# Spreading a row of maxima over all partitions: by way of DRAM instead of products with a diagonal

## The chip, the cores and the metric

The kernel runs on one core of a Trainium2 chip. The metric is the device time of one execution in microseconds; the time of a kernel is the median of several executions. A core has five engines that run their own instruction streams in order: PE (TensorE, matrix products), DVE (VectorE), ACT (ScalarE), POOL (GpSimd) and SP (SyncE), which here issues all DMAs.

## The reference

Linear attention (softmax of q over its channels, softmax of k over the sequence) is followed by a small network with the activation h - tanh(h). The inputs are q, k and v of 8 batches x 8 heads x 576 rows x 64 channels.

```python
k_s = k - np.max(k, axis=2, keepdims=True)          # over the sequence
k_s = np.exp(k_s)
k_s = k_s / (np.sum(k_s, axis=2, keepdims=True) + 1e-09)
kv = np.einsum('bhsd,bhse->bhde', k_s, v)
attn = np.einsum('bhsd,bhde->bhse', q_s, kv)        # q_s: softmax of q over d
x = attn.transpose(0, 2, 1, 3).reshape(B * S, H * D)  # 4608 x 512
h = x @ w_in                                         # 512 -> 2048
out = (h - np.tanh(h)) @ w_out                       # 2048 -> 512
```

For each batch the kernel needs the maximum over 576 rows for each of 8 x 64 = 512 columns of k, and this row of 512 numbers must stand in all 128 partitions before it can be subtracted.

## The kernel before, in words

The 4608 rows of x are cut into 9 chunks of 512. For each chunk j and each of 16 blocks f of d_ff there is a step: `ph` (12 products, x in a high and a low part against `w_i`), then the activation on ACT and DVE, ending in `gh` (ACT) and `gl` (POOL), and two steps later `po` (12 products of `gh` and `gl` with `w_o`, summed in PSUM over the 16 blocks). `ph` has two PSUM buffers, so the product of step n + 2 needs the DVE operation `t` of step n to be done.

Batches 0 and 1 and the weights are prepared under an order written out by hand (`ORDER`). From chunk 2 on, `prepare` lists the work that makes the x of a chunk and gives every piece a half step at which it is put into the program (`put(at, ...)`). There PE's and SP's order is the program's, while DVE's, ACT's and POOL's is set by a scheduler when the program is built. All engines work in order at run time: an instruction that waits holds up everything behind it on its engine, and on SP a DMA whose data aren't ready holds up all later DMAs.

For a batch b from 2 on the keys' softmax goes so: `k_load` brings k in two tiles of 256 rows and one of 64. `kv_max` (DVE) takes maxima down to a tile of 128 x 512. `kv_max_t` (PE) turns it (`pm`), `kv_row` (DVE) reduces to `mx`, 128 x 4: the 512 maxima lie down the partitions. `kv_row_h` and `kv_row_l` split `mx` into a rounded part `mh` and the rest `ml`. `kv_rows` spreads them: POOL multiplies the identity with `mh`, then with `ml`, to two tiles `d` of 128 x 512 with the numbers on a diagonal, and PE multiplies each with a matrix of ones, so that all partitions of the PSUM tile `pb` hold the row. `kv_sub` (DVE) subtracts `pb` from the three tiles of k, `kv_exp` (ACT) takes the exponent, and `kv_mm` (PE, `pk`) multiplies with v. At half step KX + 2 (= 3) of the chunk come `kv_max_t`, `kv_row`, `kv_row_h` and `kv_row_l`, at KX + 4 `kv_rows` and the subtractions.

The same DVE, POOL and SP also prepare q: `q_load`, `mq` (maxima, DVE), the subtraction (POOL, `q<-q,mq`), exponent (ACT), `sq` (sums, DVE), `qn` (POOL), then a turn on PE (`pt`) and `px`. The tile of q is single: the next `q_load` waits until the last `qn` has read it. v's first and second part share a buffer too: a memset on POOL that waits for the first `pk` products comes before the second `v_load`. The SBUF tag `qs` has three buffers, in which `km`, the two `d`, `qn` and `qs` follow one another. At the start of a chunk the four output tiles of the chunk before are copied by ACT and stored by SP (L680).

Of the kernel before, what the change touches and what calls it, by code (L numbers as in the profile page):

```python
# [10 lines left out]
F32 = mybir.dt.float32  # L11
F32R = mybir.dt.float32r
# [4 lines left out]
ALU = mybir.AluOpType  # L17
# [53 lines left out]
def attn_moe_kernel(  # L71
# [9 lines left out]
    nc = tc.nc  # L81
# [3 lines left out]
    P = 128  # L85
# [4 lines left out]
    NC = DM // P  # L90
# [15 lines left out]
    ap = ctx.enter_context(tc.tile_pool(name="ap", bufs=2))  # L106
    ps_o = ctx.enter_context(tc.tile_pool(name="ps_o", bufs=TPC, space=bass.MemoryType.PSUM))
    ps_h = ctx.enter_context(tc.tile_pool(name="ps_h", bufs=2, space=bass.MemoryType.PSUM))
    ps_m = ctx.enter_context(tc.tile_pool(name="ps_m", bufs=2, space=bass.MemoryType.PSUM))
# [4 lines left out]
    sm = ctx.enter_context(tc.tile_pool(name="sm", bufs=2))  # L114

    ident = const.tile([P, P], F32, name="ident")
# [2 lines left out]
    nc.gpsimd.tensor_copy(ident_r, ident)  # L119
    b_pa = sm.tile([P, 1], F32, name="b_pa")  # L120
    nc.gpsimd.memset(b_pa, PA)
    one = sm.tile([P, 1], F32, name="one")
    nc.gpsimd.memset(one, 1.0)
    one_r = sm.tile([P, 1], F32R, name="one_r")
    nc.gpsimd.tensor_copy(one_r, one)

    kvs = [const.tile([P, NC, D], F32, name=f"kvs{i}") for i in range(3)]

# [73 lines left out]
    def k_load(b: int, st: dict, u: int):  # L202
        if u < NKP:
            kt = ap.tile([P, H, 2, D], F32, name=f"k{b}_{u}", tag="k", bufs=NKP)
            src = k[b, :, 2 * P * u : 2 * P * (u + 1), :]
            nc.sync.dma_start(
                kt.rearrange("p h j d -> p h (j d)"), src.rearrange("h (p j) d -> p h (j d)", j=2)
            )
        else:
            kt = ap.tile([REST, H, D], F32, name=f"kr{b}", tag="kr", bufs=1)  # L210
            nc.sync.dma_start(kt, k[b, :, S - REST :, :].rearrange("h s d -> s h d"))
        st["k", u] = kt
# [30 lines left out]
    def kv_max(b: int, st: dict, n: int):  # L243
        if n == 0:
            st["km"] = km = ap.tile([P, H, D], F32, name=f"km{b}", tag="qs", bufs=3)
            kt = st["k", 0]
            nc.vector.tensor_tensor(km, kt[:, :, 0], kt[:, :, 1], op=ALU.max)
        elif n < 3:
            km = st["km"]
            nc.vector.tensor_tensor(km, km, st["k", 1][:, :, n - 1], op=ALU.max)  # L250
        else:
            km = st["km"][:REST]
            nc.vector.tensor_tensor(km, km, st["k", NKP], op=ALU.max)
# [20 lines left out]
    def kv_rows(b: int, st: dict):  # L274


        pb = ps_m.tile([P, NC, P], F32, name=f"pb{b}", tag="m")
        if b < 2:
            for a in range(NC):
                for n, m in enumerate((st["mh"], st["ml"])):  # L280
                    nc.tensor.matmul(
                        pb[:, a, :],
                        m[:, a : a + 1].broadcast_to([P, P]),
                        ident_r,
                        start=(n == 0),
                        stop=(n == 1),
                    )
        else:
            for n, m in enumerate((st["mh"], st["ml"])):
                d = ap.tile([P, NC, P], F32R, name=f"d{b}_{n}", tag="qs", bufs=3)  # L290
                nc.gpsimd.tensor_tensor(
                    d,
                    ident.unsqueeze(1).broadcast_to([P, NC, P]),
                    m.bitcast(F32).unsqueeze(2).broadcast_to([P, NC, P]),
                    op=ALU.mult,
                )
                nc.tensor.matmul(
                    pb.rearrange("p a m -> p (a m)"),
                    one_r.broadcast_to([P, P]),
                    d.rearrange("p a m -> p (a m)"),  # L300
                    start=(n == 0),
                    stop=(n == 1),
                )
        st["pb"] = pb.rearrange("p a (e d) -> p (a e) d", d=D)

    def kv_sub(b: int, st: dict, u: int):
        pb, kt = st["pb"], st["k", u]
        pb = pb.unsqueeze(2).broadcast_to([P, H, 2, D]) if u < NKP else pb[:REST]
        nc.vector.tensor_tensor(kt, kt, pb, op=ALU.subtract)

    def kv_exp(b: int, st: dict, u: int):
        nc.scalar.activation(st["k", u], st["k", u], AF.Exp)

    def kv_mm(b: int, st: dict, u: int):


        if u == 0:
            st["pk"] = ps_m.tile([P, NC, D + 2], F32, name=f"pk{b}", tag="m")
        kt, vt = st.pop(("k", u)), st.pop(("v", u))
        for j in range(2 if u < NKP else 1):  # L320
            for a, hh in [(a, hh) for a in range(NC) for hh in range(2)]:
                h = hh * NC + a
                nc.tensor.matmul(  # L323
                    st["pk"][hh * D : (hh + 1) * D, a, j : j + D + 1],
                    kt[:, h, j] if u < NKP else kt[:, h],
                    vt[:, h, j * (D + 1) : (j + 1) * (D + 1)],
                    start=(u == 0 and j == 0 and a == 0),
                    stop=(u == NKP and a == NC - 1),
                    skip_group_check=True,
                )  # L330

    def kv_den(b: int, st: dict, n: int):
        pk = st["pk"]
        if n == 0:
            st["sl"] = sm.tile([P, NC, 1], F32, name=f"sl{b}", tag="sl")
            nc.vector.tensor_scalar_add(st["sl"], pk[:, :, D + 1 : D + 2], EPS)
        elif n == 1:
            st["rs"] = sm.tile([P, NC, 1], F32, name=f"rs{b}", tag="rs")
            nc.vector.tensor_tensor(st["rs"], pk[:, :, 0:1], st["sl"], op=ALU.add)
        else:  # L340
            nc.vector.reciprocal(st["rs"], st["rs"])

    def kv_norm(b: int, st: dict):
        nc.vector.tensor_tensor(
            kvs[b % 3],
            st["pk"][:, :, 1 : D + 1],
            st["rs"].broadcast_to([P, NC, D]),
            op=ALU.mult,
        )
# [11 lines left out]
    def batches(i: int):  # L361
        (b, u), _ = tiles[i]
        return ((b - 1, 0, REST), (b, REST, P)) if u == "rest" else ((b, 0, P),)
# [146 lines left out]
    def prepare(j: int, put):  # L510

        mine = range(j * TPC, (j + 1) * TPC)
        new = {b for i in mine for b, _, _ in batches(i)}
        new -= {b for i in range(mine[0]) for b, _, _ in batches(i)}

        KX, PAIRS = 1, (16, 28)
        for b in new:
            st = {}
            for u in range(NKP + 1):
                put(0, lambda u=u: k_load(b, st, u))  # L520
            for u in (0, NKP):
                for part in (v_ones, v_load):
                    put(0, lambda u=u, part=part: part(b, st, u))
            for n in range(4):
                put(KX, lambda n=n: kv_max(b, st, n))
            for part in (kv_max_t, kv_row, kv_row_h, kv_row_l):
                put(KX + 2, lambda part=part: part(b, st))
            put(KX + 4, lambda: kv_rows(b, st))
            for u in range(NKP + 1):
                put(KX + 4, lambda u=u: kv_sub(b, st, u))  # L530
                put(KX + 4, lambda u=u: kv_exp(b, st, u))
            put(KX + 7, lambda: kv_mm(b, st, 0))
            for part in (v_ones, v_load):
                put(KX + 7, lambda part=part: part(b, st, 1))
            put(KX + 10, lambda: kv_mm(b, st, 1))
            put(KX + 10, lambda: kv_mm(b, st, NKP))
            for n in range(3):
                put(KX + 10, lambda n=n: kv_den(b, st, n))
            put(KX + 10, lambda: kv_norm(b, st))
        unit = None  # L540
        for i in mine:
            at = PAIRS[(i - mine[0]) // 2]
            turn = at - (3 if i % 2 else 5)
            if tiles[i][0] != unit:
                unit = tiles[i][0]
                if unit not in qs_of and tiles[i][1] == 0:
                    put(max(0, turn - 9), lambda unit=unit: q_load(unit))
                    put(max(2, turn - 4), lambda unit=unit: q_soft(unit))
            put(turn, lambda i=i: q_norm(i, nc.gpsimd))
            put(turn, lambda i=i: q_turn(i))  # L550
            put(turn, lambda i=i: q_keep(i))
            if i % 2:
                put(at, lambda i=i: x_mm(i - 1))
                for g in range(2):
                    for p in "hl":
                        put(at, lambda i=i, g=g, p=p: x_part(i - 1, g, p))
# [76 lines left out]
    dram = ctx.enter_context(tc.tile_pool(name="dram", bufs=1, space=bass.MemoryType.DRAM))  # L633
# [75 lines left out]
    for b in range(2):  # L709
        st = {}  # L710
# [43 lines left out]
    with tc.manual_schedule(engines={ENG.PE, ENG.DVE, ENG.Activation, ENG.Pool, ENG.SP}):  # L754
        for name in ORDER.split():
            eng = (nc.vector,) if name[-1] == "*" else ()
            name = name.rstrip("*")
# [74 lines left out]
```

## Time and profile before

| | us |
|---|---|
| median of 3 runs | 899.44 (899.38 to 899.83) |
| profiled execution, its time | 902.51 |
| its span in the trace | 900.7 |
| PE busy | 874.9 |
| DVE busy | 616.7 |
| ACT busy | 555.0 |
| POOL busy | 289.2 |

The profiled execution has a time of its own, and the trace covers its span. A busy time is the sum over an engine's instructions; PE's products overlap, so what one costs in a stream is the difference of two starts and not its duration. The row that a line of a timeline shows is: start, duration, engine, line, operation, output<-inputs, and in brackets the idle time before it and who ended it. L numbers are lines of the kernel before.

### The profile page before, as it was taken

Reading aid. Unit: us, or ns where it says so; the run is one execution under the profiler, and the core shown is the slowest. Engines: PE = TensorE matmul, PEld = TensorE weight load, DVE = VectorE, ACT = ScalarE, POOL = GpSimd, SP = SyncE. Lnnn points to the kernel's source line nnn. Section 1 sums busy time; section 2 is a strip of 40 time slices with the busy share of each in tenths; the row PEclk is TensorE's granted clock in tenths of the full one; section 3 lists DMA queues with packets and bytes.
Section 4 is the critical chain, followed back from the end, with each engine's and each line's share of the span. In section 5 each row is a group of like instructions: output and inputs, shape, how many; then the busy total and the mean of one; then the engine's idle time right before and its main releaser. Section 6 shows DMA issues by size and latency. Waiting matters only on the chain.

```text
span 900.7 us, 13173 instructions
## 1 busy us (share of the span) xinstructions
PE 874.9 (97%) x5008; PEld 716.6 (80%) x5008; DVE 616.7 (68%) x906; ACT 555.0 (62%) x967; POOL 289.2 (32%) x246
## 2 busy tenths in 40 slices
PE   5899989999999999999999999999999999999997
PEld 5777778878778888888888888888888888888886
DVE  7999988957576767567656865866765566454444
ACT  4899986655555657555646565565656566556553
POOL 4631112433144324332333332332433233222221
PEclk8999999999999999999999999999999999999999
DMA  9983301040142202300140011301100020001001
GB/s 292 306 314 118 115 9 41 24 140 2 53 100 61 69 1 82 107 24 1 47 123 7 24 47 35 107 0 48 48 24 1 1 70 12 1 1 48 1 1 47
DMA packets 79775, 57.47 MB, mean 64 GB/s; under 512 B 14688, under 2 KB 72032, under 8 KB 79712
## 3 DMA queue, kind: packets, MB, share of 16 engines
q1 hardware_dynamic: 79712, 56.63, 20.5%
q8 instruction: 39, 0.64, 0.3%
q14 instruction: 24, 0.20, 0.1%
HBM read 46.14 MB, written 10.49 MB: 63 GB/s over the span
## 4 chain that ended last, share of the span: by engine, by line
PE 78%; DVE 12%; ACT 5%; issue 2%; DMA 2%; POOL 1%; SPq 0%; DVEq 0%; ACTq 0%; POOLq 0%
PE po L651 36%; PE ph L568 36%; PE pk L323 2%; PE px L487 2%; PE pt L461 1%; DVE g L589 1%; DMA k<-in_k_dram 1%; DVE t L594 1%; DVE g L597 1%; DVE g L602 1%; ACT gh L605 1%; ACT mk L583 1%; DVE c_o L168 1%; DVE raw_i L157 1%; DVE c_i L168 1%
## 5 line engine op out<-in xcount | busy, mean ns | idle before, releaser
L651 PE MATMUL po<-w_o,gh 128*128 128x512 f32 x1152 | 358.7, 392 | 0.3 <-DVE w_o L179 0.2
L568 PE MATMUL ph<-xh,w_i 128*128 128x512 f32 x1152 | 313.4, 394 | 4.7 <-DVE t L594 2.3
L608 POOL TENSOR_TENSOR gl<-g,gh 128x512 fp32r<-128x512 f32 x128 | 171.5, 1340 | 389.3 <-ACT gh L605 367.0
L568 PEld LDWEIGHTS ph<-xh,w_i 128*128 128x128 f32 x1152 | 213.5, 188 | 49.8 <-DVE t L594 2.8
L651 PEld LDWEIGHTS po<-w_o,gh 128*128 128x128 f32 x1152 | 214.8, 188 | 47.3 <-issue 1.5
L589 DVE SCALAR_TENSOR_TENSOR g<-u,ph 128x512 f32<-128x512 f32 x144 | 98.2, 682 | 209.1 <-ACT t L583 204.7
L651 PE MATMUL po<-w_o,gl 128*128 128x512 f32 x576 | 224.5, 390 | 0.2 <-DVE gl L608 0.2
L605 ACT CAST gh<-g 128x512 fp32r<-128x512 f32 x144 | 89.5, 622 | 176.3 <-DVE g L602 168.5
L568 PE MATMUL ph<-xl,w_i 128*128 128x512 f32 x576 | 155.1, 391 | 0.0
L583 ACT ACTIVATE u<-ph 128x512 f32<-128x512 f32 x144 | 86.1, 598 | 78.4 <-PE ph L568 78.2
L597 DVE SCALAR_TENSOR_TENSOR g<-vv,g 128x512 f32<-128x512 f32 x144 | 117.4, 816 | 18.3 <-ACT vv L583 7.9
L651 PEld LDWEIGHTS po<-w_o,gl 128*128 128x128 f32 x576 | 108.3, 188 | 23.5 <-DVE gl L608 0.7
L568 PEld LDWEIGHTS ph<-xl,w_i 128*128 128x128 f32 x576 | 108.1, 188 | 23.7 <-DVE xl L508 0.5
L602 DVE COPY_PREDICATED g<-mk,t 128x512 f32<-128x512 int32 x144 | 119.6, 830 | 3.4
L583 ACT ACTIVATE mk<-ph 128x512 int32<-128x512 f32 x144 | 86.4, 600 | 36.1 <-DVE g L589 34.2
L583 ACT ACTIVATE vv<-u,b_pa 128x512 f32<-128x512 f32 x144 | 104.8, 727 | 0.7 <-DVE g L597 0.6
L594 DVE TENSOR_TENSOR t<-ph,t 128x512 f32<-128x512 f32 x144 | 98.0, 681 | 6.7 <-ACT mk L583 5.9
L583 ACT ACTIVATE t<-ph 128x512 f32<-128x512 f32 x144 | 85.6, 594 | 3.0 <-DVE g L589 3.0
L447 POOL TENSOR_TENSOR qn<-q,sq 128x512 f32<-128x512 f32 x30 | 34.6, 1153 | 27.7 <-PE pt L461 13.4
L413 POOL TENSOR_TENSOR q<-q,mq 128x1024 f32<-128x1024 f32 x14 | 28.0, 2003 | 46.4 <-DVE mq L408 44.6
L408 DVE TENSOR_REDUCE mq<-q 128x16 f32<-128x1024 f32 x15 | 18.3, 1217 | 23.3 <-DMA q<-in_q_dram 23.3
L179 POOL TENSOR_TENSOR w_i<-c_i,w_i 128x512 fp32r<-128x512 f32 x12 | 18.3, 1529 | 39.1 <-ACT w_i L175 39.1
(94 smaller groups left out, 577.4 us busy)
## 6 DMA issues: line engine op xcount, KB each, us to landing
k<-in_k_dram SPq DMA_DIRECT2D x16, 512.0 KB, 5.5
raw_i<-in_moe_w_in_dram SPq DMA_DIRECT2D x16, 512.0 KB, 6.7
raw_o<-in_moe_w_out_dram SPq DMA_DIRECT2D x16, 512.0 KB, 8.3
q<-in_q_dram SPq DMA_DIRECT2D x15, 512.0 KB, 3.9
v<-in_v_dram SPq DMA_DIRECT2D x14, 512.0 KB, 4.8
out_dram<-o SPq DMA_DIRECT2D x28, 256.0 KB, 2.2
kr<-in_k_dram SPq DMA_DIRECT2D x8, 128.0 KB, 5.2
spare_v<-in_v_dram SPq DMA_DIRECT2D x2, 512.0 KB, 7.9
```

What stands on the lines that cost most here:

```text
L179: eng.tensor_tensor(w[:, 1], st["c"].bitcast(F32), w[:, 0].bitcast(F32), op=ALU.subtract)
L413: eng.tensor_tensor(qf, qf, mq, op=ALU.subtract)
L447: eng.tensor_tensor(qn.rearrange("p a g d -> p g a d"), qt[:, :, j].rearrange("p (g a) d -> p g a d", g=2), sq[:, :, j : j + 1] .broadcast ...
L568: nc.tensor.matmul(ph, w[:, i, c], x[:, c, :], start=(n == 0), stop=(n == len(ops) - 1))
L583: nc.scalar.activation(new(tag, **of), st[src], fn, **kw)
L589: nc.vector.scalar_tensor_tensor(new("g"), st["u"], C2, st["ph"], op0=ALU.mult, op1=ALU.mult)
L594: nc.vector.tensor_tensor(st["t"], st["ph"], st["t"], op=ALU.subtract)
L597: nc.vector.scalar_tensor_tensor(st["g"], st["vv"], PB, st["g"], op0=ALU.add, op1=ALU.mult)
L602: nc.vector.copy_predicated(st["g"], st["mk"], st["t"])
L605: nc.scalar.copy(new("gh", F32R), st["g"])
L608: eng.tensor_tensor(new("gl", F32R), st["g"], st["gh"].bitcast(F32), op=ALU.subtract)
L651: nc.tensor.matmul(po[t], g[:, cols], wt["o", f][:, w], start=(begin and n == 0), stop=(end and n == 2),)
```

## The change

From batch 2 on the row of maxima is no longer made by POOL and PE. SP stores `mx` (128 x 4) to a DRAM tile `row` of 4 x 128, where the 512 numbers lie in order, and then loads this row into all partitions of an SBUF tile `rows`, 128 x 512. The load waits for the store. The split into `mh` and `ml` falls away for these batches, as do the two tiles `d`, the PSUM tile `pb` and the ones. Both DMAs are put at half step KX + 2, right behind `kv_row`. The subtractions read `rows` in SBUF instead of `pb` in PSUM. Batches 0 and 1 stay as they were.

```diff
-    one = sm.tile([P, 1], F32, name="one")
-    nc.gpsimd.memset(one, 1.0)
-    one_r = sm.tile([P, 1], F32R, name="one_r")
-    nc.gpsimd.tensor_copy(one_r, one)
...
     def kv_rows(b: int, st: dict):
-        pb = ps_m.tile([P, NC, P], F32, name=f"pb{b}", tag="m")
         if b < 2:
+            pb = ps_m.tile([P, NC, P], F32, name=f"pb{b}", tag="m")
...
         else:
-            for n, m in enumerate((st["mh"], st["ml"])):
-                d = ap.tile([P, NC, P], F32R, name=f"d{b}_{n}", tag="qs", bufs=3)
-                nc.gpsimd.tensor_tensor(
-                    d,
-                    ident.unsqueeze(1).broadcast_to([P, NC, P]),
-                    m.bitcast(F32).unsqueeze(2).broadcast_to([P, NC, P]),
-                    op=ALU.mult,
-                )
-                nc.tensor.matmul(
-                    pb.rearrange("p a m -> p (a m)"),
-                    one_r.broadcast_to([P, P]),
-                    d.rearrange("p a m -> p (a m)"),
-                    start=(n == 0),
-                    stop=(n == 1),
-                )
+            row = dram.tile([NC, P], F32, name=f"row{b}")
+            nc.sync.dma_start(row.rearrange("a p -> p a"), st["mx"])
+            pb = ap.tile([P, NC, P], F32, name=f"rows{b}", tag="qs", bufs=3)
+            nc.sync.dma_start(pb, row.unsqueeze(0).broadcast_to([P, NC, P]))
         st["pb"] = pb.rearrange("p a (e d) -> p (a e) d", d=D)
...
-            for part in (kv_max_t, kv_row, kv_row_h, kv_row_l):
+            for part in (kv_max_t, kv_row, kv_rows):
                 put(KX + 2, lambda part=part: part(b, st))
-            put(KX + 4, lambda: kv_rows(b, st))
```

The change also moves instructions on the engines that the scheduler orders. Three places follow; a number after a name tells apart tiles of one name, and L numbers of the program now are those of the changed kernel.

DVE at batch 7 (in chunk 6), from the maxima to the first operations of the step after. Before:

```order
L263 TENSOR_REDUCE mx_6095<-pm_6090 128x4
L594 TENSOR_TENSOR t_1_6051<-ph_1_6036,t_1_6051 128x512
L268 CAST mh_6097<-mx_6095 128x4
L602 COPY_PREDICATED g_1_6053<-mk_1_6057,t_1_6051 128x512
L272 TENSOR_TENSOR ml_6099<-mx_6095,mh_6097 128x4
L589 SCALAR_TENSOR_TENSOR g_2_6118<-u_2_6114,ph_2_6101 128x512
L597 SCALAR_TENSOR_TENSOR g_2_6118<-vv_2_6120,g_2_6118 128x512
L594 TENSOR_TENSOR t_2_6116<-ph_2_6101,t_2_6116 128x512
L309 TENSOR_TENSOR k_0_6007<-k_0_6007,pb_6149 128x1024
L309 TENSOR_TENSOR k_1_6009<-k_1_6009,pb_6149 128x1024
L309 TENSOR_TENSOR kr_6011<-kr_6011,pb_6149 64x512
L602 COPY_PREDICATED g_2_6118<-mk_2_6122,t_2_6116 128x512
```

Now, at the same place on DVE:

```order
L259 TENSOR_REDUCE mx_6056<-pm_6051 128x4
L578 TENSOR_TENSOR t_1_6012<-ph_1_5997,t_1_6012 128x512
L586 COPY_PREDICATED g_1_6014<-mk_1_6018,t_1_6012 128x512
L573 SCALAR_TENSOR_TENSOR g_2_6079<-u_2_6075,ph_2_6062 128x512
L581 SCALAR_TENSOR_TENSOR g_2_6079<-vv_2_6081,g_2_6079 128x512
L294 TENSOR_TENSOR k_0_5968<-k_0_5968,rows_6060 128x1024
L294 TENSOR_TENSOR k_1_5970<-k_1_5970,rows_6060 128x1024
L578 TENSOR_TENSOR t_2_6077<-ph_2_6062,t_2_6077 128x512
L294 TENSOR_TENSOR kr_5972<-kr_5972,rows_6060 64x512
L393 TENSOR_REDUCE mq_1_6220<-q_1_6092 128x16
L586 COPY_PREDICATED g_2_6079<-mk_2_6083,t_2_6077 128x512
```

The two large subtractions now stand ahead of the step's `t`, and `mq` ahead of the step's COPY_PREDICATED.

SP at batch 7, the stores of a finished chunk and what follows. Before:

```order
L680 DMA out_dram<-o_15_0_6069 128x512
L680 DMA out_dram<-o_15_1_6075 128x512
L680 DMA out_dram<-o_15_2_6081 128x512
L680 DMA out_dram<-o_15_3_6087 128x512
L393 DMA q_1_6131<-in_q_dram 128x8x128
L235 DMA v_1_6251<-in_v_dram 128x8x128
```

Now:

```order
L664 DMA out_dram<-o_15_0_6030 128x512
L664 DMA out_dram<-o_15_1_6036 128x512
L664 DMA out_dram<-o_15_2_6042 128x512
L664 DMA out_dram<-o_15_3_6048 128x512
L286 DMA row_6058<-mx_6056 128x4x1
L288 DMA rows_6060<-row_6058 128x512
L378 DMA q_1_6092<-in_q_dram 128x8x128
L231 DMA v_1_6205<-in_v_dram 128x8x128
```

The pair stands behind the four stores and ahead of the loads of q and v.

DVE at batch 2, from the subtractions on. Before:

```order
L309 TENSOR_TENSOR k_0_1691<-k_0_1691,pb_1838 128x1024
L309 TENSOR_TENSOR k_1_1693<-k_1_1693,pb_1838 128x1024
L309 TENSOR_TENSOR kr_1695<-kr_1695,pb_1838 64x512
L589 SCALAR_TENSOR_TENSOR g_14_1825<-u_14_1821,ph_14_1808 128x512
L408 TENSOR_REDUCE mq_0_1963<-q_0_1806 128x16
L597 SCALAR_TENSOR_TENSOR g_14_1825<-vv_14_1827,g_14_1825 128x512
```

Now:

```order
L294 TENSOR_TENSOR k_0_1687<-k_0_1687,rows_1788 128x1024
L294 TENSOR_TENSOR k_1_1689<-k_1_1689,rows_1788 128x1024
L294 TENSOR_TENSOR kr_1691<-kr_1691,rows_1788 64x512
L393 TENSOR_REDUCE mq_0_1952<-q_0_1802 128x16
L573 SCALAR_TENSOR_TENSOR g_14_1821<-u_14_1817,ph_14_1804 128x512
L581 SCALAR_TENSOR_TENSOR g_14_1821<-vv_14_1823,g_14_1821 128x512
```

`mq`, which waits for the load of q, now comes ahead of the step's `g`. On ACT in this place the order after q's exponent was `gh`, and is now `u`, `t`, `gh`. On POOL, `qn` loses the two `d` ahead of it. PE's order is the same but for the twelve products that fall away.

## The prediction

> **What bounds the kernel now.** I read the page's busy shares first, then the chain that ended last, then the busy times by stretch, and last the timelines around the places where a batch's maxima are spread.
>
> ```profile
> span 900.7 us, 13173 instructions
> PE 874.9 (97%) x5008; PEld 716.6 (80%) x5008; DVE 616.7 (68%) x906; ACT 555.0 (62%) x967; POOL 289.2 (32%) x246
> ...
> PE 78%; DVE 12%; ACT 5%; issue 2%; DMA 2%; POOL 1%; SPq 0%; DVEq 0%; ACTq 0%; POOLq 0%
> ...
> 150.00:200.00 50.00, 49.14 (x293) 40.15 (x291) 38.16 (x57) 29.81 (x52) 19.21 (x17) 1.00 0.18 53
> 250.00:300.00 50.00, 49.36 (x316) 40.02 (x315) 37.17 (x53) 28.61 (x48) 21.35 (x18) 1.00 0.36 92
> 600.00:700.00 100.00, 100.00 (x586) 81.95 (x586) 66.33 (x93) 59.55 (x102) 34.74 (x27) 1.00 0.09 27
> ```
>
> The first column of busy times in a stretch is PE's. Around batch 7 (600 to 700 us) PE is never idle; around batches 2 and 3 it idles 0.86 and 0.64 us. The clock granted is full in all three. So whatever leaves PE's stream shortens the program, as long as nobody makes PE wait in exchange. DVE, at 38 of 50 and 66 of 100 us, is the engine to watch: it works in order, and the change puts a DMA's landing in front of it.
>
> **What is removed from PE.** First the group, then batch 7 and batch 3 in PE's timeline (start, duration), the last line from the chain.
>
> ```profile
> L297 PE MATMUL pb<-d,one_r 128*128 128x512 f32 x12 | 4.1, 407 | 0.6 <-POOL d L291 0.6
> ...
> 632.91 0.63 PE L297 MATMUL pb<-d,one_r 128*128 128x512 f32 x2
> 633.38 1.09 PE L568 MATMUL ph<-xh,w_i 128*128 128x512 f32 x4
> ...
> 262.68 0.42 PE L297 MATMUL pb<-d,one_r 128*128 128x512 f32 x1
> 263.75 0.50 PE L297 MATMUL pb<-d,one_r 128*128 128x512 f32 x1 [0.64 <-POOL d L291]
> 264.24 2.74 PE po L651 x12
> ```
>
> The mean of 407 ns is no price: products overlap. In the stream a pair takes 633.38 - 632.91 = 0.47 us, and I use that for batches 2, 4, 5, 6 and 7: 5 x 0.47 = 2.35. In batch 3 PE waited for POOL's second diagonal between the two, so the pair cost 264.24 - 262.68 = 1.56. Together 3.91 us, all in a place where PE had other work ready behind.
>
> Batch 2 has a stall of its own, further down:
>
> ```profile
> 186.29 1.15 PE L323 MATMUL pk<-v,k 128*64 128x65 f32 x32 [0.86 <-POOL gl L608]
> 182.02 0.38 SPq L235 DMA_DIRECT2D v<-in_v_dram x1
> v<-in_v_dram SPq DMA_DIRECT2D x1, 512.0 KB, 4.2
> ```
>
> The releaser named is POOL's gl, but gl ended earlier; the load of v issued at 182.02 lands 4.2 later, at 186.2, and that is when the product starts. So the stall hangs on how early POOL gets to the memset that lets v be loaded. If that comes 1.33 us (0.86 + 0.47) earlier, the 0.86 goes too. The most that can be won is 3.91 + 0.86 = 4.77 us.
>
> **What is added: the time L from the issue of the first DMA to the landing of the second.** No transfer of 512 pieces of 4 bytes to DRAM, and no read of one 2 KB row by all partitions, is in the trace. The nearest issues from 100 to 700 us, by kind (last column: median us from issue to landing):
>
> ```profile
> out_dram<-o SPq DMA_DIRECT2D x18, 256.0 KB, 2.0
> out_dram<-o SPq DMA_DIRECT2D x4, 128.0 KB, 2.4
> q_rest<-in_q_dram SPq DMA_DIRECT2D x6, 128.0 KB, 3.2
> q<-in_q_dram SPq DMA_DIRECT2D x11, 512.0 KB, 3.9
> kr<-in_k_dram SPq DMA_DIRECT2D x6, 128.0 KB, 5.2
> ```
>
> Writing the maxima moves 8 KB. It is a store like out_dram, whose time hardly falls when its bytes are halved (2.0 and 2.4), so most of it is fixed: 2.0 below. Above, q_rest and kr have the same 512 pieces: 3.2, or 5.2 behind other loads. I take 2.2, since at this place only stores of the same kind stand in the queue. Reading it back is 256 KB in 128 rows of 2 KB: 2.0 below (a store of that shape), 3.9 above (a load of twice the bytes); I take 2.9. With two hand-overs of about 0.05, L = 5.2, bounds 4.1 and 9.2.
>
> By the Trainium skill ("DMA: Bandwidth & Descriptors", Anatomy of one DMA — SWDGE (gpsimd) path) a DMA costs about 2.0 us plus bytes at 436 GB/s; that gives an estimate of L = 4.6. The same page (Specifications) has pieces under 512 B done by read-modify-write, which speaks against this store; no row here shows a 4-byte store.
>
> **What L does in batch 7**, where four stores of outputs stand ahead on SP. DVE's, POOL's and SP's rows, and the product that needs the result:
>
> ```profile
> 626.04 3.04 SPq L680 DMA_DIRECT2D out_dram<-o  x4
> 627.62 0.69 DVE L263 TENSOR_REDUCE mx<-pm 128x4 f32<-128x512 f32 x1 [0.26 <-PE pm L259]
> 633.18 0.68 DVE L594 TENSOR_TENSOR t<-ph,t 128x512 f32<-128x512 f32 x1
> 633.79 2.33 DVE L309 TENSOR_TENSOR k<-k,pb 128x1024 f32<-128x1024 f32 x2
> 636.04 0.67 DVE L309 TENSOR_TENSOR kr<-kr,pb 64x512 f32<-64x512 f32 x1
> 636.64 0.75 DVE L602 COPY_PREDICATED g<-mk,t 128x512 f32<-128x512 int32 x1
> 637.29 1.20 DVE L408 TENSOR_REDUCE mq<-q 128x16 f32<-128x1024 f32 x1
> 638.62 1.91 POOL L413 TENSOR_TENSOR q<-q,mq 128x1024 f32<-128x1024 f32 x1 [4.21 <-DVE mq L408]
> 640.49 1.74 POOL L608 TENSOR_TENSOR gl<-g,gh 128x512 fp32r<-128x512 f32 x1
> 642.81 2.95 PE po L651 x12
> ```
>
> The maxima are ready at 628.31, but the last output's issue ends only at 629.08. So the rows arrive at x = 629.08 + L = 634.3, against 633.79 before. DVE's new order is k, k, t, kr, mq, then the copy. From start to start k, k take 2.25, t 0.61, kr 0.60, so mq starts at x + 3.46 and ends at x + 4.66; POOL subtracts until x + 6.7 and then makes gl, until x + 8.0 to x + 8.45 (1.3 alone, 1.74 in the row). ACT's gh is done before that. PE asks for this gl with its third product after 642.81, about 643.26, less the 0.47 saved: 642.8. So x may be 634.35 to 634.8, and L up to about 5.5 costs nothing; each further microsecond is one of PE. I replayed batches 3 to 6 in the same way and found them up to 0.8 us looser, so 5.5 for all five is on the safe side. SP itself loses nothing: behind the pair stands a load that POOL's qn let go only at 632.74 before.
>
> **What L does in batch 2**, where SP is free and the store goes out when the maxima are ready:
>
> ```profile
> 164.57 0.69 DVE L263 TENSOR_REDUCE mx<-pm 128x4 f32<-128x512 f32 x1
> 170.52 2.35 DVE L309 TENSOR_TENSOR k<-k,pb 128x1024 f32<-128x1024 f32 x2 [0.16 <-PE pb L297]
> 173.39 0.67 DVE L589 SCALAR_TENSOR_TENSOR g<-u,ph 128x512 f32<-128x512 f32 x1
> 175.21 1.22 DVE L408 TENSOR_REDUCE mq<-q 128x16 f32<-128x1024 f32 x1 [1.14 <-DMA q<-in_q_dram]
> 169.71 1.51 POOL L447 TENSOR_TENSOR qn<-q_rest,sq_rest 128x512 f32<-128x512 f32 x1
> 171.25 3.93 DMA q<-in_q_dram
> 176.00 0.60 ACT L583 ACTIVATE u<-ph 128x512 f32<-128x512 f32 x1 [0.42 <-PE ph L568]
> 176.49 0.59 ACT L583 ACTIVATE t<-ph 128x512 f32<-128x512 f32 x1
> ```
>
> x = 165.3 + L = 170.5, the same as before. What moves is the q load: it waited for POOL's qn, which stood behind the two diagonals (2.5 us). Without them q lands at about 172.7 and no longer holds up mq, which now comes straight after the three subtractions, at x + 2.87 = 173.4 instead of 175.21. From mq hangs the v load: POOL's subtraction, ACT's exponent, gh, gl, memset. ACT's new order puts two more steps (u and t, 0.5 each from start to start) ahead of gh. So v lands at 186.27 + (x + 2.87 - 175.21) + 1.0 = x + 14.9, and PE is there at 185.43 - 0.47 = 184.96. Up to L = 4.7 the stall is gone; at 5.2 half a microsecond of it stays.
>
> **Costed at nothing.** The casts and differences of the maxima (12 instructions on DVE) and the diagonals (12 on POOL): neither engine sets PE's pace at 600 to 700 us; what they won in batch 2 is in the sum through q. The memset and the cast of the ones at the start: I give them 0, or 0.3 us as the best case. One PSUM buffer less in use: I found no wait for it. The subtractions now read both operands from SBUF:
>
> ```profile
> 165.92 1.26 DVE L268 CAST mh<-mx 128x4 fp32r<-128x4 f32 x1
> 167.29 1.55 DVE L597 SCALAR_TENSOR_TENSOR g<-vv,g 128x512 f32<-128x512 f32 x1
> ```
>
> These two ran beside POOL's gl and diagonal. The second works on two operands in SBUF and took 1.55 us where t, with one operand in PSUM, takes 0.68 above: DVE's work on SBUF can stretch by 0.9 us while POOL runs. At the subtractions POOL has finished qn and waits for mq, so I take 0; the bound is 0.9 a batch, which counts as L + 0.9. The Trainium skill ("SBUF — State Buffer", SBUF: two separate sides) states the reason: a VectorE operation with two SBUF inputs and a GpSimd operation that reads SBUF exclude each other for a whole instruction. The two long rows fit that.
>
> **Sum.** Gain = 4.77 - max(0, L - 4.7) - 5 x max(0, L - 5.5). At L = 5.2 it is 4.77 - 0.5 = 4.3 us. The profiled execution, 902.51 us with its span of 900.7, stands 3.1 above the median of 899.44; the gain is a difference within it and I take it off the median: 899.44 - 4.3 = 895.2.
>
> **Rivals.**
> 1. The pair of DMAs is slow. For: 4-byte pieces, all partitions reading one row, kr at 5.2. Against: nothing else is in the queue, and 512 pieces in q_rest take 3.2 although two such loads run together. The gain is zero at L = 6.2; at L = 7 the sum is 4.77 - 2.3 - 7.5 = -5.0, 904.4 us. It decides through one mechanism: DVE stands at the subtractions, gl is late, PE waits, in every batch from 3 on.
> 2. L about 6, or the port stretches the subtractions by 0.9 at L = 5.2: the gain is 4.77 - 1.3 - 2.5 = 1.0, 898.5 us, no measurable change. If read-modify-write of pieces under 512 B, as the Trainium skill has it on the DMA page, adds a microsecond to the store, this is where it would end.
> 3. The products were free because the work behind them comes no sooner: 899.4. Against: PE has no idle time at 600 to 700 us and both neighbours of the pair start at once.
>
> **Chances.** A change below 0.2% (1.8 us), about what a measurement can tell from none, needs L between 5.9 and 6.5 or rival 3. Forecast, L up to 5.9: 0.72. Rival 2 with 3: 0.13 (0.09 and 0.04). Rival 1, L over 6.5: 0.15. The best case, L = 4.4, is 899.44 - 4.8 = 894.7, with 0.3 for the start 894.4, and I set the end at 894.3. Leaving out rival 1 and a sliver of the rest, the range ends at 899.5; the forecast's own range is 894.3 to 897.6.
>
> **What would show it.** After: no L297 group, no d on POOL; row landing at 2.0 to 2.5 and rows at 2.4 to 3.2; batch 7's first subtraction near 634.3 less what was won before; PE still idle-free at batches 4 to 7; the pk stall of batch 2 under 0.6. Wrong if PE shows waits for gl or for t in batches 3 to 7, if DVE's wait for rows is over 2 us, or if the subtractions take over 1.3 us each.

## The result and the profile after

The changed kernel takes 951.14 us (median of 4 runs, 947.79 to 951.90) against 899.63 (4 runs, 899.38 to 901.99): a ratio of 1.0555, interval 1.0539 to 1.057. It is 51.5 us slower; 895.2 was forecast and 899.5 was the end of the range. The profiled execution took 951.79 us with a span of 950.0.

First the page: busy times, the chain by engine, and the DVE group and the two DMA groups that are new (the store's row from the view of DMA issues, 100 to 800 us).

```profile
PE 887.3 (93%) x4996; PEld 724.7 (76%) x4996; DVE 610.8 (64%) x894; ACT 555.5 (58%) x967; POOL 271.3 (29%) x232
...
PE 69%; DMA 10%; DVE 9%; ACT 5%; issue 3%; SPq 2%; POOL 0%; ACTq 0%; DVEq 0%; POOLq 0%
...
L294 DVE TENSOR_TENSOR k<-k,rows 128x1024 f32<-128x1024 f32 x12 | 14.2, 1222 | 55.0 <-DMA rows<-row 55.0
...
rows<-row SPq DMA_DIRECT2D x6, 256.0 KB, 5.0
row<-mx SPq DMA_DIRECT2D x6, 2.0 KB, 8.3
```

The subtractions themselves take 1222 ns, as before. DVE idles 55.0 us ahead of them, 9.2 a batch, always for the load of the rows. The store of 2 KB lands after 8.3 us, the load after 5.0: L is 13.3, where 5.2 was forecast and 9.2 was the upper bound. DMA, 2% of the chain before, has 10% of it.

The waits, by engine (line waited for, total, times, longest), and PE's busy time in the stretches that were shown of before:

```profile
DVE k L294 <- DMA rows<-row: 55.0, 6, 9.7
PE ph L552 <- DVE t L578: 20.3, 4, 7.2
PE pk L308 <- ACT k L297: 18.7, 6, 7.0
...
150.00:200.00 50.00, 43.39 (x257) 35.47 (x256) 33.54 (x51) 25.20 (x44) 13.89 (x13) 0.93 0.11 32
250.00:300.00 50.00, 43.02 (x248) 35.26 (x248) 30.44 (x44) 23.21 (x39) 13.63 (x13) 0.90 0.30 76
600.00:700.00 100.00, 92.77 (x505) 75.64 (x504) 62.86 (x86) 55.71 (x96) 29.18 (x23) 0.97 0.19 51
```

PE, which never idled at 600 to 700 us, now idles 7.2 us there, and the clock granted (third number from the end) falls below 1.00 in each of the three stretches. Over the whole span PE idles 62.7 us (950.0 less 887.3) where it idled 25.8 before, and it is busy 12.4 us longer although it has twelve products fewer.

Batch 7 shows the whole of it: SP, DVE and PE.

```profile
669.86 0.41 SPq L286 DMA_DIRECT2D row<-mx  x1
678.21 0.33 SPq L288 DMA_DIRECT2D rows<-row  x1
...
668.28 0.69 DVE L259 TENSOR_REDUCE mx<-pm 128x4 f32<-128x512 f32 x1 [0.25 <-PE pm L255]
683.38 2.36 DVE L294 TENSOR_TENSOR k<-k,rows 128x1024 f32<-128x1024 f32 x2 [9.39 <-DMA rows<-row]
685.66 0.68 DVE L578 TENSOR_TENSOR t<-ph,t 128x512 f32<-128x512 f32 x1
...
686.40 2.07 PE L552 MATMUL ph<-xh,w_i 128*128 128x512 f32 x4 [7.23 <-DVE t L578]
```

The store is issued at 669.86; SP stands until 678.21 for its landing; the rows land at 683.3; DVE has stood since 674.0. The step's `t` stands behind the subtractions on DVE, and PE's product waits for `t`.

Why the store takes so long: busy share of the DMA engines (last but one) in the stretches after an issue at 163.69 (batch 2), whose landing lets SP go on at 171.83.

```profile
164.00:165.00 1.00, 1.00 (x6) 0.82 (x5) 0.63 (x2) 1.00 (x3) 0.74 (x1) 1.00 0.25 2
165.00:166.00 1.00, 1.00 (x7) 0.80 (x6) 1.00 (x1) 0.23 (x1) 1.00 (x2) 1.00 0.00 0
...
167.00:171.70 4.70, 4.70 (x23) 3.88 (x22) 0.61 (x1) 1.71 (x3) 1.30 (x2) 1.00 0.00 0
```

The last number is GB/s: the 2 KB are moved within 1.3 us of the issue. Then the profile shows no busy DMA engine for over 6 us until the landing is reported. So the time doesn't go into the moving of the pieces, but into what follows until the landing is reported. The Trainium skill ("DMA: Bandwidth & Descriptors", Anatomy of one DMA — SWDGE (gpsimd) path) says of the fixed cost that it is mostly the receipt of the write, which can be surprisingly long towards HBM. That section is about DMAs issued by GpSimd, and this one is issued by SP; the trace fits it in kind, with some 6 us in place of the page's 2.0, but it doesn't show what this time is spent on.

### The profile page after: what moved, and what is told of

Its sections match the earlier page's. It is cut to its first block, busy times and chain, and to the rows that moved or that the text cites. A ratio compares the mean times of both kernels' runs of the same rounds, so it can differ in the third digit from the quotient of the medians.

```text
span 950.0 us, 13133 instructions
## 1 busy us (share of the span) xinstructions
PE 887.3 (93%) x4996; PEld 724.7 (76%) x4996; DVE 610.8 (64%) x894; ACT 555.5 (58%) x967; POOL 271.3 (29%) x232
## 4 chain that ended last, share of the span: by engine, by line
PE 69%; DMA 10%; DVE 9%; ACT 5%; issue 3%; SPq 2%; POOL 0%; ACTq 0%; DVEq 0%; POOLq 0%
PE po L635 33%; PE ph L552 32%; DMA row<-mx 4%; DMA rows<-row 3%; PE pk L308 2%; PE px L472 1%; PE pt L446 1%; DVE k L294 1%; DMA k<-in_k_dram 1%; DVE t L578 1%; DMA raw_o<-in_moe_w_out_dram 1%; DVE g L573 1%; DMA raw_i<-in_moe_w_in_dram 1%; DVE g L581 1%; DVE g L586 1%
## 5 line engine op out<-in xcount | busy, mean ns | idle before, releaser
L635 PE MATMUL po<-w_o,gh 128*128 128x512 f32 x1152 | 363.3, 397 | 3.4 <-ACT gh L589 3.1
L552 PE MATMUL ph<-xh,w_i 128*128 128x512 f32 x1152 | 316.2, 397 | 22.7 <-DVE t L578 20.3
L592 POOL TENSOR_TENSOR gl<-g,gh 128x512 fp32r<-128x512 f32 x128 | 169.5, 1324 | 440.4 <-ACT gh L589 418.0
L635 PEld LDWEIGHTS po<-w_o,gh 128*128 128x128 f32 x1152 | 217.7, 191 | 51.2 <-ACT gh L589 3.5
L635 PE MATMUL po<-w_o,gl 128*128 128x512 f32 x576 | 227.5, 395 | 0.5 <-DVE gl L592 0.2
L581 DVE SCALAR_TENSOR_TENSOR g<-vv,g 128x512 f32<-128x512 f32 x144 | 119.5, 830 | 17.9 <-ACT vv L567 7.5
L586 DVE COPY_PREDICATED g<-mk,t 128x512 f32<-128x512 int32 x144 | 116.8, 811 | 3.6
L297 ACT ACTIVATE k<-k 128x1024 f32<-128x1024 f32 x16 | 16.9, 1056 | 62.2 <-DVE k L294 61.9
L294 DVE TENSOR_TENSOR k<-k,rows 128x1024 f32<-128x1024 f32 x12 | 14.2, 1222 | 55.0 <-DMA rows<-row 55.0
```

The lines of the kernel that those rows point to most:

```text
L552: nc.tensor.matmul(ph, w[:, i, c], x[:, c, :], start=(n == 0), stop=(n == len(ops) - 1))
L581: nc.vector.scalar_tensor_tensor(st["g"], st["vv"], PB, st["g"], op0=ALU.add, op1=ALU.mult)
L586: nc.vector.copy_predicated(st["g"], st["mk"], st["t"])
L592: eng.tensor_tensor(new("gl", F32R), st["g"], st["gh"].bitcast(F32), op=ALU.subtract)
L635: nc.tensor.matmul(po[t], g[:, cols], wt["o", f][:, w], start=(begin and n == 0), stop=(end and n == 2),)
```

## The experiments

Each was compared with the kernel before on the same chip: 900.59 us (15 runs) for e1 to e4, 900.73 (15) for e5 to e8, 901.24 (9) for e9 and e10, 900.98 (21) for e11 and e12.

### The store and the load by themselves (e1_probe, e8_stores)

To the kernel before, chains of DMAs are added on SP in stretches in which it has nothing to do. No engine waits for them; each overwrites or reads the tile of the one ahead, so that the next issue shows when the one ahead landed. Two of the stores, as an example:

```diff
+    t = store("sta", [NC, P], lambda t: t.rearrange("a p -> p a"), dt[:, :NC])  # 512 x 4 B, adjacent
+    go(dt, t.rearrange("a p -> (a p)").unsqueeze(0).broadcast_to([P, DM]))
+    store("std", [P, NC, 16], lambda t: t[:, :, 0:1], dt[:, :NC].unsqueeze(2))  # 512 x 4 B, 64 B apart
```

> The kernel before, with chains of extra DMAs on SP in the quiet stretches after the loads of k (nobody waits for them but the next DMA of the chain). Stores from SBUF to DRAM: sta 512 pieces of 4 B to neighbouring addresses as in the change; stb 128 pieces of 16 B; std 512 pieces of 4 B, 64 B apart; ste 512 of 4 B, 512 B apart; stf 512 of 64 B; sti 512 of 256 B; sth 128 of 4 B; stg 4 of 512 B; stc 128 of 2 KB. Loads of 128 x 2 KB: one row for all partitions (fresh from sta, stb, stg; old; from the input k) and 128 different rows. Theory A, pieces under a line's size are written by read-modify-write and neighbours in one line wait for each other: sta 8.3, stb 2 to 4, std and ste 2 to 3.5, sth 3 to 8, the others about 2. Theory B, each piece under 512 B costs by itself whatever its place: sta, std, ste, stf all 7 to 8.5, stb and sth 3 to 4. Theory C, any small store to DRAM is acknowledged late: all of them near 8 but stc. Loads: if one row read by all partitions is what makes 5.0, every broadcast takes about 5 and different rows 2.5 to 3; if it is that the row was just written, only the fresh ones do. Time: 899 to 901, no change, if DMAs off the path cost nothing.

> The kernel before, with chains of DMAs that nobody waits for, in stretches in which SP has nothing to do; the time stays at about 900.6. Theory C (small pieces that go to the same 64 bytes of DRAM are written one after another, about 0.45 us each): 512 pieces of 4 bytes land in 4 to 5 us when they lie 8 bytes apart, 2.5 to 3.2 at 16 and 2.2 to 3.1 at 32; 16 adjacent pieces of 4 bytes take 7 to 8, as 256 do; 128 pieces 64 bytes apart 2 to 2.5; 256 pieces of 8 bytes, adjacent, 4 to 5. Theory D (each piece under 512 bytes has a price): the time goes by their number, 16 pieces about 2, 512 pieces about 8 at every distance. The load that reads a row just stored takes about 5 us by both, and a load of other data behind such a store about 3.

Measured: e1_probe 900.79 us (10 runs), ratio 1.0005, interval 0.9992 to 1.0017: this traffic alone costs nothing that the runs can tell. e8_stores ran once, at 902.08, which decides nothing about the time; only its landings are used. SP's timeline of the first, then of the second (there a digit at the end of a name is left out: `sp` is 512 pieces 8 bytes apart, `s` 16 adjacent pieces, `sother` and `sagain` 512 adjacent ones):

```profile
297.05 0.37 SPq L520 DMA_DIRECT2D sta<-probe  x1
305.74 0.34 SPq L527 DMA_DIRECT2D probe<-sta  x1
310.79 0.33 SPq L520 DMA_DIRECT2D stb<-probe  x1
...
477.92 0.32 SPq L520 DMA_DIRECT2D stg<-probe  x1
479.11 0.35 SPq L544 DMA_DIRECT2D probe<-stg  x1
```

```profile
298.95 0.37 SPq L520 DMA_DIRECT2D sp<-probe  x1
302.33 0.34 SPq L534 DMA_DIRECT2D probe<-in_k_dram  x1
...
378.79 0.34 SPq L520 DMA_DIRECT2D s<-probe  x1
380.26 0.35 SPq L542 DMA_DIRECT2D probe<-in_k_dram  x1
...
581.26 0.37 SPq L520 DMA_DIRECT2D sother<-probe  x1
591.83 0.34 SPq L557 DMA_DIRECT2D probe<-in_k_dram  x1
594.94 0.37 SPq L520 DMA_DIRECT2D sagain<-probe  x1
```

The store of the change lands after 305.74 - 297.05 = 8.7 us, and later after 10.6; four pieces of 512 bytes (`stg`) after 1.2. All of them, from such differences:

| store to DRAM | us |
|---|---|
| 512 x 4 B, adjacent | 8.4 to 10.6 (4 times) |
| 256 and 128 x 4 B, adjacent | 7.7 and 7.1 |
| 16 x 4 B, adjacent | 1.5 |
| 512 x 4 B, 8, 16, 32, 64, 512 B apart | 3.4, 2.8, 2.1, 3.0, 2.2 |
| 128 x 4 B, 64 B apart | 1.5 |
| 256 x 8 B and 128 x 16 B, adjacent | 3.3 and 2.5 |
| 512 x 64 B and 512 x 256 B | 2.5 and 1.9 |
| 4 x 512 B | 1.2 |
| 128 x 2 KB | 2.0 |

(The stores 64 and 512 bytes apart also lie in another order: a partition's four pieces follow one another.) The number of pieces doesn't set the price, and neither does their size by itself: 512 pieces of 4 bytes cost 2.1 us at 32 bytes apart. Of the forms tried, only many pieces of 4 bytes that touch each other are slow. In e1_probe theory A met nearly all its times; B fell with the spread pieces, C with the 16-byte and 512-byte ones. In e8_stores theory C had 16 adjacent pieces, one block of 64 bytes, at 7 to 8 us; they took 1.5, so it fell in that form. Theory D had 512 pieces at about 8 us at every distance, and fell with those apart. What happens in the memory stays open, also for theory A, whose mechanism no run shows. As for the load, one row to all partitions takes 310.79 - 305.74 = 5.05 us when it was just stored in this way (4.1 and 5.4 in the second kernel), but 3.1 when it is one that nobody wrote (594.94 - 591.83, right behind such a store) or was stored long before (3.2; 4.5 once, behind loads of v), and 3.1 and 3.0 when it was just stored as 128 pieces of 16 bytes or 4 of 512. So reading what was just written in adjacent 4-byte pieces costs 1 to 2 us more.

### Stores of larger pieces (e4_16, e6_turn)

e4_16 stores 128 pieces of 16 bytes, which leaves the row in another order, so that every subtraction is done in two parts. e6_turn turns the maxima on PE first:

```diff
-            row = dram.tile([NC, P], F32, name=f"row{b}")
-            nc.sync.dma_start(row.rearrange("a p -> p a"), st["mx"])
+            turned = ps_m.tile([NC, P], F32, name=f"turned{b}", tag="m")
+            nc.tensor.transpose(turned, st["mx"], ident)
+            line_of = sm.tile([NC, P], F32, name=f"line{b}", tag="line", bufs=1)
+            nc.vector.tensor_copy(line_of, turned)
+            row = dram.tile([NC, P], F32, name=f"row{b}")
+            nc.sync.dma_start(row, line_of)
```

> The changed kernel with one thing changed: the maxima are stored as they lie, 128 pieces of 16 B, and the subtraction (two instructions in place of one) reads the row in the other order. Theory A: the store falls from 8.3 to 2 to 4, L from 13.3 to 7 to 9, and the time to 905 to 920. Theory C: 945 or more.

> The changed kernel, but the maxima are first turned by one small product on PE and copied to 4 partitions, so that the store moves 4 pieces of 512 bytes in place of 512 of 4. Theory A (the store of small neighbouring pieces is what is slow): the store lands in under 1.5 us, the load in 3 to 5, L is 4.5 to 6.5 behind the copy, DVE waits 0 to 3 us at a batch's subtractions, and the time is 898 to 912 us. Rival (a store to DRAM that is read back at once is slow whatever its pieces): the store takes 5 us or more, and the time is over 925.

Measured: e4_16 918.44 us, ratio 1.0197 (1.0169 to 1.0226); the store lands after 2.0, the load after 4.3, DVE waits 13.6 us in all, and its subtractions take twice 1.07 us in place of once 1.22. The time lies within theory A's range, the store at its lower end and L = 6.3 below its 7 to 9; the loss of 17.9 us is more than the 13.6 of waiting, and the doubled subtractions are what else the edit adds. e6_turn 900.91 us, ratio 1.0003 (0.999 to 1.0016). Its waits and loads, and its PE at 600 to 700 us:

```profile
DVE k L298 <- DMA rows<-row: 11.1, 6, 4.5
...
rows<-row SPq DMA_DIRECT2D x6, 256.0 KB, 3.8
...
600.00:700.00 100.00, 100.00 (x588) 81.87 (x586) 66.93 (x91) 59.02 (x102) 31.19 (x25) 1.00 0.10 30
```

The same way through DRAM, with the same read right behind the write, costs nothing once the store's pieces are large. Theory A held but for DVE's waits in batches 2 and 3 (4.3 and 4.5 us where it had at most 3; 0.3 to 0.8 in the others). The loss is gone, and DVE's wait for the rows fell from 55.0 to 11.1. The order made at build differs too: the subtractions stand a few operations later on DVE, but by an estimate from batch 7, a pair of 13.3 us would leave DVE standing for 9 us there too (store issued at 629.46, DVE free at 633.4). With store and load at 1.2 and 3.8, L is 5.0, near the forecast's 5.2; but the forecast's gain of 4.3 us isn't there.

### The removal alone (e2_none)

```diff
-            nc.sync.dma_start(row.rearrange("a p -> p a"), st["mx"])
-            nc.sync.dma_start(pb, row.unsqueeze(0).broadcast_to([P, NC, P]))
+            st["pb"] = ident[:, :D].unsqueeze(1).broadcast_to([P, H, D])
```

> The changed kernel without the spreading: neither DMAs nor products; a part of the identity is subtracted instead of the maxima, and the rest stays. It measures the term of the sum for what was removed: the prediction's 4.8, so 894.7 (893.5 to 896). Rival, the products were free: 899.4. If the slower time of the changed kernel came from DVE's new order and not from the landing, this would stay above 920.

Measured: 903.70 us (6 runs, 901.31 to 907.86), ratio 1.004 (1.0014 to 1.0066): nothing to wait for, and still no gain. It is even 3.1 us slower; the profiled execution, 901.49, is one of the fastest, so the trace may not show all of that. Where `pk` of batches 5 and 7 starts in the kernel before, then in e2_none, then e2_none's new waits of PE at 150 to 180 us:

```profile
450.25 1.15 PE L323 MATMUL pk<-v,k 128*64 128x65 f32 x32
641.66 1.15 PE L323 MATMUL pk<-v,k 128*64 128x65 f32 x32
```

```profile
450.07 1.15 PE L306 MATMUL pk<-v,k 128*64 128x65 f32 x32
640.67 1.15 PE L306 MATMUL pk<-v,k 128*64 128x65 f32 x32
...
PE po L633 <- POOL gl L590: 1.6, 1, 1.6
PE po L633 <- ACT gh L587: 1.3, 1, 1.3
```

A batch takes 191.41 / 2 = 95.7 us before and 190.60 / 2 = 95.3 without the products: 0.4, near the 0.47 of the forecast. What doesn't come is the rest. The subtractions no longer depend on the maxima here, and at batch 2 they stand ahead of them on DVE (155.08 and 159.81, `mx` at 162.98), between the operations of a step and before its COPY_PREDICATED. PE stands 2.9 us there for `gh` and `gl`, for which it didn't wait before. The 0.86 us for the load of v is gone, as forecast. So this run has a DVE order of its own: it prices the removed products, but not the order of the changed kernel.

### The same slow pair, out of the way (e3_late, e5_early, e9_hidden, e11_hidden456)

If DVE's standing is the whole cost, it must go when the pair of 13.3 us lies ahead of need. e3_late holds the subtractions and q's maxima behind a later step; e5_early makes the maxima four half steps sooner and holds the subtractions in their old place; e9_hidden also clears SP's queue; e11_hidden456 does so for batches 4 to 6 alone. The core of them:

```diff
+        with tc.issue_after(copied[-1]):   # behind the COPY_PREDICATED of the latest step
             nc.vector.tensor_tensor(kt, kt, pb, op=ALU.subtract)
...
-                put(KX, lambda n=n: kv_max(b, st, n))
+                put(KX - 4, lambda n=n: kv_max(b, st, n))
-                put(KX + 2, lambda part=part: part(b, st))
+                put(KX - 2, lambda part=part: part(b, st))      # turn, reduce, store
+            put(ROWS, lambda: kv_rows(b, st, 1))                # the load: e9, e11
```

> The changed kernel with both DMAs, but the subtractions, and the maxima of q that wait for a load behind the pair on SP, are held behind a later step's copy on DVE (about 15 us after the maxima in place of 5), and the products with v four half steps later. Theory, the whole loss is the wait for the landing in DVE's order: back to 894 to 897, with DVE's wait for rows under 1 us a batch, and PE busy 100% in the stretches of batches 4 to 7. Rival, the DMAs cost by themselves (SP held, contention): 920 or more.

> Batches 0 to 2 as before. From batch 3 on the keys' maxima, their store and the load of the rows are put four half steps earlier, and the subtractions are held by an order on DVE behind the step in which they stood before, so that at least 13 us lie between the store's issue and their place. Theory A (all that the change costs is that DVE stands at the subtractions until a pair of 13.3 us has landed): DVE's wait for rows falls from 55.0 us to under 5 in all, PE is idle-free again at batches 4 to 7, and the time is 896 to 902 us: 900.6 less at most 5 x 0.47, give or take 3 for the other order. Rival B (the subtractions from SBUF, the traffic of the pair or the queue behind it cost time of their own): over 915 us with no wait for rows.

> As e5_early, with SP's queue cleared around the pair: the loads of v's first and last part and of the chunk's first q come ahead of the store of the maxima, and the load of the rows is put two half steps behind the store, so that SP doesn't stand for the landing. The subtractions are held three steps (some 17 us) behind the maxima, against 13.3 us for the slow pair. Theory A (the pair costs what waits for it and nothing else): DVE waits under 5 us in all for rows, mq for q under 20, PE is idle-free at batches 4 to 7 and a batch takes 95.2 to 95.4 us from pk to pk in place of 95.7; the time is 897 to 901.5 us. Rival B (the pair, or reading the rows from SBUF, has a cost of its own): over 905 us.

> As e9_hidden, for batches 4, 5 and 6 alone, in which e9_hidden showed no wait for the rows; batches 2, 3 and 7 are spread by products as in the kernel before. Theory A (the slow pair costs only what stands for it): no wait for rows, no wait of more than 1 us on PE in batches 4 to 6, and the time is that of before less up to 3 x 0.4: 898.5 to 901.5 us. Rival B (the pair or the operands in SBUF have a price of their own, or SP's queue lets something else wait): 903 us or more.

Measured: 947.86 us (ratio 1.0529, 1.0497 to 1.0561), 961.50 (1.0679, 1.0665 to 1.0694), 925.82 (1.0269, 1.0252 to 1.0286) and 901.98 (1.0014, 1.0005 to 1.0023). The first three missed what theory A expected, and their times lie where the rivals had them. The main waits of each, in this order (before, DVE waits 23.3 us for q in the whole span, 4.6 at most at once):

```profile
DVE k L300 <- DMA rows<-row: 0.9, 1, 0.9
PE pt L453 <- POOL qn L439: 34.2, 10, 6.4
```

```profile
DVE mq L421 <- DMA q<-in_q_dram: 59.3, 12, 14.7
PE po L669 <- ACT o L696: 26.8, 6, 8.8
...
SPq L277 <- DVE mx L263: 194.8, 5, 53.6
SPq L279 <- DMA row<-mx: 41.1, 5, 8.5
```

```profile
DVE mq L424 <- DMA q<-in_q_dram: 37.3, 12, 16.1
PE ph L590 <- DVE t L616: 11.1, 3, 8.0
PE pm L259 <- DVE km L253: 6.3, 1, 6.3
```

```profile
row<-mx SPq DMA_DIRECT2D x3, 2.0 KB, 8.6
PE po L674 <- ACT o L701: 0.8, 2, 0.6
```

In none of them does DVE wait for the rows any more (0.9 us in all in e3_late), so the wait itself was moved each time; it came back elsewhere. In e3_late q's maxima, held with the rest, made `qn` late, and PE waits for it. In e5_early SP stands first until the maxima are there (53.6 us once) and then for the landing, and the load of q and the stores of outputs stand behind it: DVE waits for q, and PE waits for the copies of outputs (`o`), whose buffers the stores hold. In e9_hidden this is left in batch 3 (16.1 us), and in batch 7 PE waits 2.7 us for `k`; in 4 to 6 there is no wait of a microsecond on PE. e11_hidden456 keeps only those three: with a store that still lands after 8.6 the loss of some 9 us a batch is gone from each of them, and 1.0 us (0.45 to 2.1) over before is left, some of it 0.8 us in which PE waits for `o`. It is half a microsecond over the range that theory A gave; rival B's 903 isn't reached. The 1.2 us that its removed products should have given are missing too, so the three hidden pairs cost some 2 us. So a transfer of 13.6 us can be hidden almost free, though it pays in SP's queue as well as on DVE.

### Is the half clock a cost of its own? (e7_fill, e10_fill)

```diff
+            fill = {3: 25, 4: 16, 5: 25, 6: 9, 7: 25}     # e7_fill: 64, 42, 64, 24, 64
+            if b in fill:
+                put(KX + 6, lambda: warm(fill[b]))        # products of the identity with itself
             put(KX + 7, lambda: kv_mm(b, st, 0))
```

> The changed kernel with 64, 42, 64, 24 and 64 products of the identity with itself (about 0.088 us each, 22.7 us in all; their result is not used) on PE ahead of the place at which it waits in batches 3 to 7. Theory A (an idle PE is granted half the clock for some microseconds afterwards): the products fill most of the idle time, the clock stays at 1.00 behind them, the 32 products of pk take about 1.15 us in place of 2.00, and the time falls by 8 to 16 us to 935 to 943. Rival B (the clock falls for another reason, or there is no more to gain than idle time): the time stays at 948 to 953 or grows, and pk still takes 2.00.

> As e7_fill, with the fillers' number set by what one takes there (0.226 us): 25, 16, 25, 9 and 25 products in batches 3 to 7, 22.6 us in all, within the idle time. Theory A (an idle PE is granted half the clock afterwards): the same waits end as before, but the products behind them run at full clock; the time falls by 6 to 12 us, to 939 to 945, although PE has more to do. Rival B: 948 or more.

Measured: 967.19 us (ratio 1.074, 1.0723 to 1.0758) and 953.47 (1.0582, 1.0565 to 1.0599). In e7_fill one product took 0.226 us and not 0.088 (64 of them 14.45; the profile counts each as two), so it filled too much. PE at batch 3, in the changed kernel and then in e10_fill:

```profile
280.77 2.00 PE L308 MATMUL pk<-v,k 128*64 128x65 f32 x32 [6.98 <-ACT k L297]
...
281.00:282.00 1.00, 1.00 (x22) 1.00 (x22) 1.00 (x2) 1.00 (x2) 0.00 (x0) 0.50 0.00 0
```

```profile
275.48 5.74 PE L196 MATMUL warm<-ident 128*128 128x128 f32 x50
282.69 1.15 PE L308 MATMUL pk<-v,k 128*64 128x65 f32 x32 [1.47 <-ACT k L297]
287.65 1.21 PE L555 MATMUL ph<-xh,w_i 128*128 128x512 f32 x4 [0.82 <-DVE t L581]
```

After 7 us of idling the clock granted is 0.50 and the 32 products take 2.00 us; with the fillers it is 1.00 and they take 1.15, as before the change. So idling does cost the clock. The Trainium skill ("TensorE: Matmul & The Clock Gate", Part 1: The HAM clock gate) has the same, half rate after an idle window of about 3.4 us; in the traces looked at here each idle time from 3.8 us on did it, and of shorter ones some (2.38 and 2.72 in e9_hidden) and others not (2.81 in the changed kernel, 3.53 in e10_fill). But the time didn't fall: 953.5 against 951.1, with ratios to before whose intervals overlap. Two limits: the mean clock came back only from 0.969 to 0.982 (0.994 before), and DVE's wait for the rows was 58.4 us in e10_fill's trace, 3.4 more than in the changed kernel. So a gain of up to some 3 us may be hidden there, but not the 6 to 12 of theory A, which is wrong in its second half. Where the clock is back, PE comes sooner to the next thing that isn't ready (`ph` waits 0.82 for `t`, which it didn't before): DVE was behind as well, and most of the slower clock hid in its lateness.

### The version that came out of it (e12_turn4567)

The turned store for batches 4 to 7, products for 0 to 3:

```diff
+        if b >= 4:
+            ...                                    # as in e6_turn
+            return
         pb = ps_m.tile([P, NC, P], F32, name=f"pb{b}", tag="m")
```

> The turned store of e6_turn for batches 4 to 7 alone; batches 2 and 3 are spread by products as before, so that the 2.1 us which PE waited in batch 3 of e6_turn are gone. The removed pair of products is worth 0.47 us a batch and the turn costs about 0.1: 4 x 0.35 = 1.4 us less than before, 898.5 to 900.5 us, if the maxima's way by DRAM is as short as there. If the gain in e6_turn's batches was an accident of order, the time stays at 900.5 to 902.

Measured: 898.76 us (11 runs, 897.53 to 900.28) against 900.98 (21 runs): ratio 0.9978, interval 0.9969 to 0.9987, some 2 us faster than the kernel before and than e6_turn, and at the lower end of what was expected. Its `pk` of batches 5 and 7, and DVE's wait for rows:

```profile
448.44 1.15 PE L334 MATMUL pk<-v,k 128*64 128x65 f32 x32
639.15 1.15 PE L334 MATMUL pk<-v,k 128*64 128x65 f32 x32
...
DVE k L320 <- DMA rows<-row: 2.9, 4, 1.2
```

A batch takes 190.71 / 2 = 95.35 us, 0.35 less than before, as expected (0.47 less 0.1 for the turn). Four such batches make 1.4 of the 2.2 us between the medians; the rest is not explained.

## Why the prediction was wrong

- **The store, 2.2 us with 5.2 as the upper bound: it took 8.3.** This is the step that failed. No row showed 4-byte pieces, and the bound was taken from loads with the same number of pieces. The runs show that number isn't the measure: 512 pieces of 4 bytes land after 2.1 or 8.7 us depending on whether they touch. "Bounds from both sides" held only as far as the nearest rows were alike, and the value that was taken lay near the best case. The prediction also put the store at 8 KB; it is 2.0 KB. The sentence on read-modify-write pointed to this store, but gave it a microsecond and 9% of chance. The estimate of L = 4.6 beside the sum came from a section on DMAs that GpSimd issues, and no run bears it out for this store.
- **The load, 2.9 with 3.9 as the bound: 5.0.** About 3.1 is what reading one row by all partitions takes alone, and 3.8 in e6_turn; the rest comes with a row just stored in adjacent 4-byte pieces.
- **The slack: 5.5 us free, then one for one.** With L = 13.3 the sum gives 4.77 - 8.6 - 39.0 = -42.8, or 942 us; 951 was measured. DVE's 55.0 us of waiting less some 2 us of saved products give 53, near the 51.5, so in waits of 9 us little or no slack shows; how much is not separated here from the slower clock. For shorter waits the slack was there: some 1 us in e12_turn4567 cost nothing, and 4.3 and 4.5 us in batches 2 and 3 of e6_turn showed as 2.1 us of PE waiting for `k`.
- **The gain, 4.77.** The 0.47 a batch for the products was about right (0.4 in e2_none; 0.35 in e12_turn4567, which also pays for the turn). The 2.9 us in batches 2 and 3 came as a gain in no run: in e2_none waits for `gh` and `gl` took their place, in an order that is its own, so how much the changed kernel's order would have left of them stays open.
- **SP loses nothing.** This held in the changed kernel (DVE waits 19.9 us for q, 23.3 before). It failed as a rule: when the pair stood ahead of q's load and the outputs, SP's standing was the cost (e5_early).
- **The subtractions from SBUF, 0, bound 0.9 a batch.** They took 1.22 us in the changed kernel; in e11_hidden456, beside POOL's work, up to 2.33, at no visible cost to PE. Of the two long rows in the prediction the cast reads one operand, so only the other is a case of the sentence cited there.
- **Rival 1** had the mechanism: DVE stands at the subtractions, and PE waits. What PE waits for is another, though: `t` (20.3 us) and `k` (18.7), and `gl` hardly at all (0.2). Batch 2 is hit as well, not only those from 3 on. Its price was for L = 7, and its chance of 0.15 was too small, since the store's unknown had no upper row at all.

## What to carry to other kernels

Before a small array is sent through DRAM, look at how its pieces lie there: a transpose on the way (one product and a copy) turned a store of 8.3 us into one of 1.2 here. Where no row of the trace is like an operation in the very thing that is odd about it, an upper bound from other rows isn't one, and the rival that it is slow deserves much more than its share. And count a landing twice, once at the engine that needs the data, once in the queue that has to stand for it before its next DMA.

## What the runs showed of the hardware

- A store of 128 to 512 adjacent 4-byte pieces to DRAM is reported 7.1 to 10.6 us after its issue, though the pieces of the one looked at are moved within 1.3 us; 8 bytes apart it takes 3.4, and 16 adjacent pieces 1.5.
- A row read by all partitions right after such a store takes 5.0 us (4.1 to 5.4), one that wasn't just written 3.1, and one just stored in pieces of 16 or 512 bytes 3.1 or 3.0.
- After idle times of 3.8 us and more PE is granted half the clock (0.50) for some microseconds (`pk` 2.00 in place of 1.15 us), after some of 2.4 to 3.5 us too. Filling most of the idle time brought no measurable gain here.
